# Moving sums of a fused attention and mixture-of-experts kernel from VectorE to GpSimd, with folding and packing on one two-bank PSUM tile

## The chip, the cores and the metric

The kernel runs on one core of one Trainium2 chip. Its engines are TensorE (PE, with its weight loads shown as PEld), VectorE (DVE), ScalarE (ACT), GpSimd (POOL) and SyncE (SP), which here only issues transfers. The metric is device time in microseconds; lower is better.

## The reference, cut to what matters

```python
batch, n_heads, seq, head_dim, n_pack = 8, 8, 576, 64, 32      # N, D, E, F = 4608, 512, 4, 1024

def sm_attn(qq, kk, vv):
    s = scale * np.matmul(qq, kk.transpose(0, 1, 3, 2))
    a = np.exp(s - np.max(s, axis=-1, keepdims=True))
    a = a / (np.sum(a, axis=-1, keepdims=True) + 1e-09)
    return np.matmul(a, vv)

p_packed = sm_attn(p, k, v)                  # 32 packing vectors attend to 576 keys, per head
x = sm_attn(q, p_packed, p_packed)           # the tokens attend to the packed vectors
p = domain_probs / (domain_probs.sum(-1, keepdims=True) + 1e-09)
for e in range(E):
    out += p[:, e:e + 1] * (np.maximum(x @ w1[e], 0.0) @ w2[e])
```

All of it is float32. An image is one entry of the batch: 576 tokens, 8 heads.

## The kernel before

**The work.** The token attention's result is never formed. The packed vectors are folded into the first weights instead (`g_form`: packed vectors times `w1`, per head), and the token probabilities (`xs`) are multiplied with that. The second matrix product is done with Winograd's form of Strassen's scheme: 2x2 blocks, seven products in the order `ORDER = ["a11", "s3", "s1", "s2", "a22", "s4", "a12"]`, with sums of the activation blocks (`s1` to `s4`, VectorE, line 316), sums of the weight blocks (`t1` to `t4`, line 354) and sums of the results (`finish`, line 391). Every operand of a large matmul is split into a high and a low part: the high part is a cast on ScalarE (`hi_of`, line 110), the low part a subtraction on GpSimd or VectorE (`lo_of`, line 115), and three matmuls make one product.

**The loops.** The main loop runs over `units`: four image pairs (`sb`), eight chunks of 512 hidden features (`ch`, two to an expert), and the two images of the pair, the even one first. A unit does the seven products of its chunk; between them it does four groups of matmuls for the next unit's hidden blocks (`mm1_group`, after products 1, 3, 4 and 6, evicted on VectorE at line 299 with ReLU and the token's expert probability). A product's PSUM tile is copied to an accumulator (ScalarE, line 380, chunk 0), added to it (VectorE, line 382, chunks 1 to 6) or handed to `finish` (chunk 7), which forms the block sums on VectorE and stores the four output blocks. The operand of product i+2 (`s_operand`) is prepared while product i runs; it lands in a tile `st`, of which there are four (`bufs=4`). The large PSUM tiles `dbl` are three of two banks each; the small ones `aux` are two of one bank.

**Beside them.** In even units the folding for the next chunk comes after products 2 and 5 (`next(gsteps)`), each step filling one `aux` tile per image. The next image pair's attention is spread over the loop as `back`: one packing unit (`pack_unit`, half the heads of one image) in each even unit of chunks 1 to 4, one token unit (`tok_unit`) in the even units of chunks 5 and 6 and in both units of chunk 7. A generator's `yield` ends the part done in one product step. In the first image pair, odd units also form the next chunk's weight operands (`t_form`), which `t_store` then saves to DRAM for the later image pairs (`t_load`).

**The start.** Before the loop, the first two images' packing and token units, the first folding and the first weight sums run interleaved. `norm_probs` loads the expert probabilities `dp`, normalises them on VectorE and stores them to DRAM (`pnd`), from where `load_probs` reads them back broadcast to all partitions. All transfers are issued on SP's queue.

**The order.** The order of instructions on TensorE is written by hand in part (`together`, `on_pe`). Otherwise each engine's order and all waits come from a scheduler that goes through the program with estimated durations and may bring an instruction forward that is ready; each engine then runs its list in order.

Of the kernel before, what the change touches and what calls it, by code (L numbers as in the profile page):

```python
# [16 lines left out]
P = 128  # L17
# [21 lines left out]
def attention_moe(ctx: ExitStack, tc: tile.TileContext, q, k, v, p, dp, w1, w2, out):  # L39
# [12 lines left out]
    ps_aux = pool("ps_aux", 2, space=PSUM)  # L52
# [30 lines left out]
    def aux():  # L83
        return ps_aux.tile([P, 512], F32, name="aux")
# [32 lines left out]
    def norm_probs():  # L117
        pb = const.tile([P, E, TP], F32, name="pb")
        nc.sync.dma_start(out=pb, in_=dp)
        ps = const.tile([P, TP, 1], F32, name="psum_e")  # L120
        nc.vector.tensor_reduce(out=ps, in_=pb.rearrange("p e t -> p t e"), axis=AX.X, op=ALU.add)
        nc.vector.tensor_scalar_add(ps, ps, 1e-9)
        nc.vector.reciprocal(out=ps, in_=ps)
        nc.vector.tensor_tensor(
            out=pb, in0=pb, in1=ps.rearrange("p t o -> p o t").broadcast_to([P, E, TP]), op=ALU.mult
        )
        nc.sync.dma_start(out=pnd.rearrange("e (p t) -> p e t", p=P), in_=pb)

    def pack_unit(b, g, new):
        pd = pbd[b % 2]  # L130
        if g == 0:
            pt = small.tile([P, NPAIR, NPK], F32, name="pt", bufs=1)
            nc.sync.dma_start(out=pt, in_=p[b])
            for hh in range(2):
                nc.gpsimd.tensor_copy(
                    out=pd[hh * D:(hh + 1) * D, :, hh * NPK:(hh + 1) * NPK], in_=pt[hh * D:(hh + 1) * D]
                )
        kt = new([P, 2, S], "kt")
        nc.sync.dma_start(out=kt, in_=k[b][:, 2 * g:2 * g + 2, :])
        vt = new([P, len(SC), 4 * D], "vt")  # L140
# [31 lines left out]
        for c in range(nfull):  # L172
            tr(out=ps[:, c * P:(c + 1) * P], in_=a1[:, c * P:(c + 1) * P], identity=ident)
        nc.scalar.copy(out=at[:, 0:nfull, :], in_=ps.rearrange("p (c s) -> p c s", s=P))
        ps = aux()
        r = S - nfull * P
        tr(out=ps[0:r, 0:P], in_=a1[:, nfull * P:S], identity=ident)
        nc.scalar.copy(out=at[0:r, nfull, :], in_=ps[0:r, 0:P])
        yield
        ps = aux()  # L180
        for c, (_, n) in enumerate(SC):
            for h in range(4):
                mm(
                    out=ps[h * NPK:(h + 1) * NPK, 0:D], lhsT=at[0:n, c, h * NPK:(h + 1) * NPK],
# [3 lines left out]
        nc.vector.tensor_scalar_mul(ppn, ps[:, 0:D], rs)  # L188
        yield
        ps = aux()  # L190
        tr(out=ps[0:D, 0:P], in_=ppn, identity=ident)
        psv = ps[0:D, 0:P].rearrange("p (j h n) -> p j h n", j=2, h=2)
# [9 lines left out]
    def tok_unit(b, g, new):  # L202
# [20 lines left out]
        nc.vector.tensor_tensor(out=a2, in0=a2, in1=m2.broadcast_to([P, S // 32, NPK]), op=ALU.subtract)  # L223
# [6 lines left out]
        nc.vector.tensor_tensor(out=a2, in0=a2, in1=s2.broadcast_to([P, S // 32, NPK]), op=ALU.mult)  # L230
# [18 lines left out]
    def g_form(bs, ch, raws):  # L249

        for g in range(NG):
            pss = {b: aux() for b in bs}
# [81 lines left out]
    def t_form(ch, new, eng):  # L334
# [15 lines left out]
        for i, name in enumerate(ORDER):  # L350
            n = of[name]
            if n in how:
                t = new([P, 2, DH], {"t1": "at", "t2": "a1", "t3": "a1", "t4": "at"}[n])
                eng.tensor_tensor(out=t, in0=blk[how[n][0]], in1=blk[how[n][1]], op=ALU.subtract)
# [31 lines left out]
    def finish(b, name, psv):  # L386
# [5 lines left out]

        def store(t, r, n):
# [12 lines left out]
        if name == "a11":  # L406
            add(m["s2"], m["s2"], t)
            add(m["a12"], m["a12"], t)
        elif name == "s2":
            add(m["s3"], m["s3"], t)  # L410
            add(m["s4"], m["s4"], t)
            add(m["s4"], m["s4"], m["s1"])
            add(m["s1"], m["s1"], m["s3"])
# [31 lines left out]
    with ExitStack() as first:  # L445
# [10 lines left out]
        toks = [tok_unit(b, g, unit_tile(2 * b + g)) for b in range(2) for g in range(NG)]  # L456
        forms = t_form(0, form_tile, nc.gpsimd)
        for i in range(2):
# [6 lines left out]
        for i in range(2, 4):  # L465
            next(packs[i])
        norm_probs()
        next(forms)
        drain(wavefront(packs[:2], 1))
        for b in range(2):  # L470
            load_probs(b, 0)
# [19 lines left out]
    for u, (sb, ch, b) in enumerate(units):  # L491
# [3 lines left out]
        back = nothing  # L495
        if sb + 1 < SB:
# [5 lines left out]
            elif ch == 7:  # L502
                back = tok_unit(nb + 1, b % 2, att_tile)
# [6 lines left out]
        tsteps = t_form(ch + 1, att_tile, nc.vector) if forming else nothing  # L510
        next(tsteps, None)
        for i in range(NPROD):
# [12 lines left out]
            next(back, None)  # L525
            next(tsteps, None)
# [4 lines left out]
        drain(back)  # L531
# [39 lines left out]
```

## Time and profile before

| | |
|---|---|
| median of three timed runs | 1383.59 us (1379.76 to 1385.15) |
| profiled execution | 1386.64 us |
| its span, first to last instruction | 1384.9 us |
| TensorE, weight loads | busy 1312.6 us (95%), 1192.3 us (86%) |
| VectorE, ScalarE, GpSimd | busy 984.0 us (71%), 475.0 us (34%), 804.0 us (58%) |
| transfers | 208.92 MB, mean 151 GB/s |
| TensorE's granted clock, mean over the span | 0.982 of full speed |

The share of an engine is an average over stages with different limits; the stretches of time in the rows below split it. A row of instructions names line, engine, operation and `out<-in` by the program's tiles, then shape and count. Idle time before an instruction is put down to what released it last.

### The profile page before, as it was taken

Reading aid. Unit: us, or ns where it says so; the run is one execution under the profiler, and the core shown is the slowest. Engines: PE = TensorE matmul, PEld = TensorE weight load, DVE = VectorE, ACT = ScalarE, POOL = GpSimd, SP = SyncE. Lnnn points to the kernel's source line nnn. Section 1 sums busy time; section 2 is a strip of 40 time slices with the busy share of each in tenths; the row PEclk is TensorE's granted clock in tenths of the full one; section 3 lists DMA queues with packets and bytes.
Section 4 is the critical chain, followed back from the end, with each engine's and each line's share of the span. In section 5 each row is a group of like instructions: output and inputs, shape, how many; then the busy total and the mean of one; then the engine's idle time right before and its main releaser. Section 6 shows DMA issues by size and latency. Waiting matters only on the chain.

```text
span 1384.9 us, 26088 instructions
## 1 busy us (share of the span) xinstructions
PE 1312.6 (95%) x10464; PEld 1192.3 (86%) x10464; DVE 984.0 (71%) x1380; ACT 475.0 (34%) x786; POOL 804.0 (58%) x548
## 2 busy tenths in 40 slices
PE   5699999999889999999998999999998899999997
PEld 2488898888888889899987998889997799999997
DVE  4757778788994666667798466666779656666668
ACT  2354343434325333233323433333332342332331
POOL 2656887777846445555645544455565455555555
PEclk9789999999999999999999999999999999999999
DMA  8525454444553444444445443445444344443421
GB/s 279 209 94 176 169 183 168 166 166 143 182 188 122 144 145 158 157 159 144 132 152 174 133 164 135 133 139 163 148 146 151 111 145 132 146 146 131 138 92 69
DMA packets 84630, 208.92 MB, mean 151 GB/s; under 512 B 8608, under 2 KB 27168, under 8 KB 84512
## 3 DMA queue, kind: packets, MB, share of 16 engines
q1 hardware_dynamic: 84512, 207.27, 44.5%
q8 instruction: 83, 1.36, 0.4%
q14 instruction: 35, 0.29, 0.1%
HBM read 168.37 MB, written 38.87 MB: 150 GB/s over the span
## 4 chain that ended last, share of the span: by engine, by line
PE 76%; DVE 16%; DMA 3%; issue 2%; POOL 1%; ACT 1%; DVEq 0%; SPq 0%; ACTq 0%
PE dbl L67 71%; DVE acc L391 5%; PE aux L75 4%; DVE sblk L316 4%; DVE ablk L299 2%; DMA kt<-in_w 1%; DVE ghl L115 1%; DVE acc L382 1%; DVE a L223 1%; DMA pb<-in_dp 1%; POOL xl L115 1%; PE aux L70 1%; DMA kt<-in_q 1%; DVE s L227 0%; DVE a L219 0%
## 5 line engine op out<-in xcount | busy, mean ns | idle before, releaser
L67 PEld LDWEIGHTS dbl<-st,tt 128*128 128x128 f32 x5376 | 736.1, 189 | 93.1 <-issue 61.4
L67 PE MATMUL dbl<-st,tt 128*128 128x288 f32 x5376 | 791.3, 299 | 23.2 <-DVE acc L391 6.6
L115 POOL TENSOR_TENSOR st<-sblk,st 128x576 fp32r<-128x576 f32 x256 | 397.7, 1559 | 292.3 <-ACT st L110 288.5
L67 PE MATMUL dbl<-xh,ghl 128*128 128x288 f32 x2048 | 419.8, 297 | 0.0
L115 POOL TENSOR_TENSOR st<-ablk,st 128x576 fp32r<-128x576 f32 x192 | 286.3, 1491 | 228.4 <-ACT st L110 193.1
L67 PEld LDWEIGHTS dbl<-xh,ghl 128*128 128x128 f32 x2048 | 333.4, 191 | 0.0
L299 DVE SCALAR_TENSOR_TENSOR ablk<-dbl,pbt 128x576 f32<-128x576 f32 x256 | 192.6, 752 | 188.8 <-PE dbl L67 188.7
L67 PE MATMUL dbl<-xl,ghl 128*128 128x288 f32 x1024 | 306.5, 299 | 17.3 <-POOL xl L115 15.5
L382 DVE TENSOR_TENSOR acc<-dbl,acc 128x576 f32<-128x576 f32 x336 | 253.2, 754 | 90.3 <-PE dbl L67 89.4
L110 ACT CAST st<-sblk 128x576 fp32r<-128x576 f32 x256 | 173.0, 676 | 356.3 <-DVE sblk L316 232.3
L110 ACT CAST st<-ablk 128x576 fp32r<-128x576 f32 x192 | 129.7, 675 | 261.6 <-PE dbl L67 241.2
L67 PEld LDWEIGHTS dbl<-xl,ghl 128*128 128x128 f32 x1024 | 195.2, 191 | 20.1 <-POOL xl L115 16.7
L316 DVE TENSOR_TENSOR sblk<-ablk 128x576 f32<-128x576 f32 x128 | 116.0, 906 | 10.7 <-POOL st L115 0.5
L115 DVE TENSOR_TENSOR ghl<-aux,ghl 128x512 fp32r<-128x512 f32 x128 | 83.3, 684 | 53.1 <-ACT ghl L110 53.1
L75 PE MATMUL aux<-wraw,ppbd 64*32 64x512 f32 x1024 | 85.9, 621 | 1.9 <-DVE ppbd L195 1.8
L110 ACT CAST ghl<-aux 128x512 fp32r<-128x512 f32 x128 | 69.0, 588 | 49.9 <-PE aux L75 49.9
L316 DVE TENSOR_TENSOR sblk<-ablk,sblk 128x576 f32<-128x576 f32 x64 | 65.4, 1022 | 6.5 <-POOL st L115 0.8
L391 DVE TENSOR_TENSOR acc<-acc,acc 128x576 f32<-128x576 f32 x56 | 58.1, 1069 | 0.2
L316 DVE TENSOR_TENSOR sblk<-sblk,ablk 128x576 f32<-128x576 f32 x64 | 55.7, 871 | 2.0
L380 ACT COPY acc<-dbl 128x576 f32<-128x576 f32 x56 | 35.7, 639 | 57.3 <-PE dbl L67 57.3
L391 DVE TENSOR_TENSOR acc<-dbl,acc 128x576 f32<-128x576 f32 x48 | 35.4, 742 | 1.7 <-PE dbl L67 1.7
L75 PEld LDWEIGHTS aux<-wraw,ppbd 64*32 64x32 f32 x1024 | 14.3, 106 | 23.4 <-issue 15.5
(66 smaller groups left out, 496.2 us busy)
## 6 DMA issues: line engine op xcount, KB each, us to landing
tt<-td SPq DMA_DIRECT2D x168, 512.0 KB, 3.8
wraw<-in_w SPq DMA_DIRECT2D x128, 256.0 KB, 3.0
td<-tt SPq DMA_DIRECT2D x56, 512.0 KB, 2.6
kt<-in_k SPq DMA_DIRECT2D x16, 576.0 KB, 3.8
kt<-in_q SPq DMA_DIRECT2D x16, 576.0 KB, 3.6
pbt<-pnd SPq DMA_DIRECT2D x32, 288.0 KB, 3.9
out<-acc SPq DMA_DIRECT2D x32, 288.0 KB, 2.6
vt<-in_v SPq DMA_DIRECT2D x16, 512.0 KB, 3.8
```

Of the source, the lines that this page charges most:

```text
L67: on_pe(nc.tensor.matmul(**kw))
L70: on_pe(nc.tensor.transpose(**kw))
L75: ins = nc.tensor.matmul(**kw).ins
L110: nc.scalar.copy(out=dst, in_=src)
L115: eng.tensor_tensor(out=dst, in0=src, in1=hi.bitcast(F32), op=ALU.subtract)
L223: nc.vector.tensor_tensor(out=a2, in0=a2, in1=m2.broadcast_to([P, S // 32, NPK]), op=ALU.subtract)
L299: nc.vector.scalar_tensor_tensor(out=a, in0=ps[:, :, 0:HS], scalar=0.0, in1=pbt[b][:, ts].rearrange("p (o t) -> p o t", o=1).broadcast_to( ...
L316: nc.vector.tensor_tensor(out=t, in0=blk(x), in1=blk(y), op=op)
L380: nc.scalar.copy(out=accs[b, i], in_=psv)
L382: nc.vector.tensor_tensor(out=accs[b, i], in0=psv, in1=accs[b, i], op=ALU.add)
L391: nc.vector.tensor_tensor(out=dst, in0=x, in1=y, op=op)
```

## The change

Folding and packing take their PSUM from one tile of two banks in place of two tiles of one bank. A folding step uses one bank for each image of the pair; packing puts the four full transposes into the first bank and the short one into the second before both are copied out. The expert probabilities are loaded and normalised first, with transfers issued on ScalarE's queue; the key loads of two packing units go ahead of their value loads, for which `pack_unit` has one more `yield`. The packing vectors are copied on ScalarE in place of GpSimd. In the start, the second token unit has its subtraction and its multiplication on GpSimd. The weight sums `t1` and `t3` go from VectorE to GpSimd. In `finish`, the sums in which both operands are accumulators go to GpSimd (`side`), except for the last image, and the two additions to `s4` change places. At chunk 7, the two token units of an image form one chain over both units, without a drain between them, so that the second begins in the even unit.

```diff
-    ps_aux = pool("ps_aux", 2, space=PSUM)
+    ps_aux = pool("ps_aux", 1, space=PSUM)
...
-        return ps_aux.tile([P, 512], F32, name="aux")
+        return ps_aux.tile([P, 2, 512], F32, name="aux")
...
     def norm_probs():
         pb = const.tile([P, E, TP], F32, name="pb")
-        nc.sync.dma_start(out=pb, in_=dp)
+        nc.scalar.dma_start(out=pb, in_=dp)
...
-        nc.sync.dma_start(out=pnd.rearrange("e (p t) -> p e t", p=P), in_=pb)
+        nc.scalar.dma_start(out=pnd.rearrange("e (p t) -> p e t", p=P), in_=pb)
...
-                nc.gpsimd.tensor_copy(
+                nc.scalar.copy(
                     out=pd[hh * D:(hh + 1) * D, :, hh * NPK:(hh + 1) * NPK], in_=pt[hh * D:(hh + 1) * D]
...
         nc.sync.dma_start(out=kt, in_=k[b][:, 2 * g:2 * g + 2, :])
+        yield
         vt = new([P, len(SC), 4 * D], "vt")
...
-            tr(out=ps[:, c * P:(c + 1) * P], in_=a1[:, c * P:(c + 1) * P], identity=ident)
-        nc.scalar.copy(out=at[:, 0:nfull, :], in_=ps.rearrange("p (c s) -> p c s", s=P))
-        ps = aux()
+            tr(out=ps[:, 0, c * P:(c + 1) * P], in_=a1[:, c * P:(c + 1) * P], identity=ident)
         r = S - nfull * P
-        tr(out=ps[0:r, 0:P], in_=a1[:, nfull * P:S], identity=ident)
-        nc.scalar.copy(out=at[0:r, nfull, :], in_=ps[0:r, 0:P])
+        tr(out=ps[0:r, 1, 0:P], in_=a1[:, nfull * P:S], identity=ident)
+        nc.scalar.copy(out=at[:, 0:nfull, :], in_=ps[:, 0].rearrange("p (c s) -> p c s", s=P))
+        nc.scalar.copy(out=at[0:r, nfull, :], in_=ps[0:r, 1, 0:P])
...
-    def tok_unit(b, g, new):
+    def tok_unit(b, g, new, eng=nc.vector):
...
-        nc.vector.tensor_tensor(out=a2, in0=a2, in1=m2.broadcast_to([P, S // 32, NPK]), op=ALU.subtract)
+        eng.tensor_tensor(out=a2, in0=a2, in1=m2.broadcast_to([P, S // 32, NPK]), op=ALU.subtract)
...
-        nc.vector.tensor_tensor(out=a2, in0=a2, in1=s2.broadcast_to([P, S // 32, NPK]), op=ALU.mult)
+        eng.tensor_tensor(out=a2, in0=a2, in1=s2.broadcast_to([P, S // 32, NPK]), op=ALU.mult)
...
         for g in range(NG):
-            pss = {b: aux() for b in bs}
+            ps = aux()
+            pss = {b: ps[:, b % 2] for b in bs}
...
-                eng.tensor_tensor(out=t, in0=blk[how[n][0]], in1=blk[how[n][1]], op=ALU.subtract)
+                eng[n].tensor_tensor(out=t, in0=blk[how[n][0]], in1=blk[how[n][1]], op=ALU.subtract)
...
+        def side(dst, x, y, op=ALU.add):
+            (nc.vector if b == B - 1 else nc.gpsimd).tensor_tensor(out=dst, in0=x, in1=y, op=op)
+
...
         if name == "a11":
-            add(m["s2"], m["s2"], t)
-            add(m["a12"], m["a12"], t)
+            side(m["s2"], m["s2"], t)
+            side(m["a12"], m["a12"], t)
         elif name == "s2":
-            add(m["s3"], m["s3"], t)
-            add(m["s4"], m["s4"], t)
-            add(m["s4"], m["s4"], m["s1"])
-            add(m["s1"], m["s1"], m["s3"])
+            side(m["s3"], m["s3"], t)
+            side(m["s4"], m["s4"], m["s1"])
+            side(m["s4"], m["s4"], t)
+            side(m["s1"], m["s1"], m["s3"])
...
-        toks = [tok_unit(b, g, unit_tile(2 * b + g)) for b in range(2) for g in range(NG)]
-        forms = t_form(0, form_tile, nc.gpsimd)
-        for i in range(2):
+        toks = [
+            tok_unit(b, g, unit_tile(2 * b + g), nc.gpsimd if (b, g) == (0, 1) else nc.vector)
+            for b in range(2) for g in range(NG)
+        ]
+        forms = t_form(0, form_tile, {n: nc.gpsimd for n in ("t1", "t2", "t3", "t4")})
+        norm_probs()
+        for i in (0, 1, 0, 1):
             next(packs[i])
...
-        for i in range(2, 4):
+        for i in (2, 3, 2, 3):
             next(packs[i])
-        norm_probs()
+        for b in range(2):
+            load_probs(b, 0)
...
-        back = nothing
+        if not (ch == 7 and odd):
+            back = nothing
...
-            elif ch == 7:
-                back = tok_unit(nb + 1, b % 2, att_tile)
+            elif ch == 7 and not odd:
+                back = chain(*[tok_unit(nb + 1, g, att_tile) for g in range(NG)])
...
-        tsteps = t_form(ch + 1, att_tile, nc.vector) if forming else nothing
+        tsteps = t_form(ch + 1, att_tile, {"t1": nc.gpsimd, "t2": nc.vector, "t3": nc.gpsimd, "t4": nc.vector}) if forming else nothing
...
             next(back, None)
+            if i == 0 and ch <= 4:
+                next(back, None)
...
-        drain(back)
+        if not (ch == 7 and not odd):
+            drain(back)
```

## Rows read from the trace of the kernel before

**Rows 1.** The page, busy time of each engine, its share of the span and its instructions.

```profile
PE 1312.6 (95%) x10464; PEld 1192.3 (86%) x10464; DVE 984.0 (71%) x1380; ACT 475.0 (34%) x786; POOL 804.0 (58%) x548
```

**Rows 2.** The page, the chain of work that ended last, shares of the span by engine.

```profile
PE 76%; DVE 16%; DMA 3%; issue 2%; POOL 1%; ACT 1%; DVEq 0%; SPq 0%; ACTq 0%
```

**Rows 3.** Busy time in stretches of the span (us from its start): length, then each engine's busy us and its number of instructions, then TensorE's granted clock, the share of the DMA engines, GB/s. From the top: the start; an odd unit of the first image pair that forms weight sums; a pair of units with a packing unit; one with a token unit; the pair at the end of the second image pair; the pair after it; a pair with nothing beside it; the last pair.

```profile
0.00:71.00 71.00, 40.60 (x353) 26.07 (x353) 42.84 (x85) 22.90 (x44) 34.72 (x37) 0.85 0.70 238
...
302.00:324.50 22.50, 19.95 (x139) 19.75 (x138) 20.84 (x23) 8.30 (x15) 20.21 (x14) 0.92 0.44 159
...
588.00:629.70 41.70, 41.54 (x355) 37.47 (x356) 27.25 (x42) 12.41 (x22) 20.44 (x14) 1.00 0.45 149
629.70:668.60 38.90, 38.90 (x313) 36.10 (x320) 29.32 (x43) 12.65 (x20) 23.29 (x15) 1.00 0.46 147
...
707.40:756.70 49.30, 41.20 (x313) 36.46 (x316) 45.49 (x59) 16.08 (x26) 26.78 (x17) 0.99 0.51 173
...
756.70:796.80 40.10, 40.10 (x313) 36.47 (x320) 18.36 (x26) 17.50 (x30) 19.53 (x14) 0.97 0.40 130
...
1129.60:1167.10 37.50, 37.50 (x304) 35.49 (x310) 24.82 (x34) 11.61 (x18) 20.86 (x14) 1.00 0.42 135
1348.00:1384.90 36.90, 29.60 (x219) 28.95 (x218) 31.36 (x38) 6.75 (x10) 19.42 (x11) 0.94 0.19 65
```

**Rows 4.** Groups of instructions in the stretch 707.4 to 756.7 us: line, engine, operation, tiles, shape and count, then busy us, mean ns of one, and idle time before them with its releaser.

```profile
L115 POOL TENSOR_TENSOR st<-sblk,st 128x576 fp32r<-128x576 f32 x8 | 13.1, 1647 | 15.3 <-ACT st L110 15.3
L391 DVE TENSOR_TENSOR acc<-acc,acc 128x576 f32<-128x576 f32 x12 | 11.6, 997 | 0.0
L115 POOL TENSOR_TENSOR st<-ablk,st 128x576 fp32r<-128x576 f32 x7 | 11.1, 1585 | 7.6 <-ACT st L110 7.6
...
L115 POOL TENSOR_TENSOR xl<-at,xh 128x576 fp32r<-128x576 f32 x2 | 3.7, 1866 | 0.9 <-ACT xh L110 0.9
```

**Rows 5.** Who waited for whom in the stretch 707.4 to 756.7 us: total us, times, longest us.

```profile
POOL st L115 <- ACT st L110: 22.9, 9, 5.5
...
PE dbl L67 <- DVE ablk L299: 2.3, 2, 2.0
...
PE dbl L67 <- DVE acc L391: 2.1, 3, 1.5
PE dbl L67 <- POOL xl L115: 2.0, 1, 2.0
```

**Rows 6.** Single instructions of the last pair in order of time: start us, us, engine, line, operation.

```profile
1355.62 1.44 POOL L115 TENSOR_TENSOR st<-ablk,st 128x576 fp32r<-128x576 f32 x1 [0.82 <-ACT st L110]
...
1357.20 2.67 DVE L391 TENSOR_TENSOR acc<-acc,acc 128x576 f32<-128x576 f32 x2
1357.21 2.05 POOL L115 TENSOR_TENSOR st<-ablk,st 128x576 fp32r<-128x576 f32 x1 [0.15 <-ACT st L110]
...
1360.46 1.41 DVE L391 TENSOR_TENSOR acc<-acc,acc 128x576 f32<-128x576 f32 x2
...
1375.13 3.43 PE L67 MATMUL dbl<-st,tt 128*128 128x288 f32 x24 [0.42 <-DVE acc L391]
```

**Rows 7.** Weight sums: the groups of the whole span on VectorE (`t1`, `t3`) and on GpSimd (in the start), then, from the view of waits, those of TensorE and of its weight loads in the stretch 292 to 377 us, which has the last two pairs that form weight sums.

```profile
L354 DVE TENSOR_TENSOR at<-kt 128x512 f32<-128x512 f32 x7 | 7.3, 1037 | 1.3 <-POOL xl L115 1.3
L354 DVE TENSOR_TENSOR a<-vt,kt 128x512 f32<-128x512 f32 x7 | 5.6, 799 | 2.8 <-DMA vt<-in_w 2.8
L354 POOL TENSOR_TENSOR sblk<-st 128x512 f32<-128x512 f32 x2 | 3.1, 1552 | 0.0
...
PE dbl L67 <- DVE acc L382: 5.1, 2, 2.5
...
PEld dbl L67 <- POOL st L115: 7.6, 5, 2.8
```

**Rows 8.** Instructions of the start in order of time.

```profile
5.13 2.19 PE L67 MATMUL dbl<-kt,pbd 128*64 128x288 f32 x8 [5.13 <-DMA kt<-in_k]
9.01 2.19 PE L67 MATMUL dbl<-kt,pbd 128*64 128x288 f32 x8 [1.69 <-DMA kt<-in_k]
...
15.29 0.26 ACT L178 COPY at<-aux 64x128 f32<-64x128 f32 x1
15.66 0.59 SPq L119 DMA_DIRECT2D pb<-in_dp  x1
25.51 0.40 DVE L121 TENSOR_REDUCE psum_e<-pb 128x36 f32<-128x144 f32 x1 [1.64 <-DMA pb<-in_dp]
27.54 1.28 DVE L124 TENSOR_TENSOR pb<-pb,psum_e 128x144 f32<-128x144 f32 x1
33.92 1.52 DVE L223 TENSOR_TENSOR a<-a,m 128x576 f32<-128x576 f32 x1
46.82 1.40 POOL L115 TENSOR_TENSOR xl<-at,xh 128x576 fp32r<-128x576 f32 x1
```

**Rows 9.** The small PSUM tiles in a pair with a packing unit, in order of time: the read-out of the first folding step, the transposes, the packing copies, the next folding step.

```profile
589.73 1.29 DVE L115 TENSOR_TENSOR ghl<-aux,ghl 128x512 fp32r<-128x512 f32 x2 [0.70 <-ACT ghl L110]
593.02 0.60 PE L70 MATMUL aux<-ident,a 128*128 128x128 f32 x4
599.13 2.00 PE L75 MATMUL aux<-wraw,ppbd 64*32 64x512 f32 x16
599.46 0.44 DVE L195 COPY ppbd<-aux 64x64 f32<-64x64 f32 x2
```

More of the change, by code (lines that the diff above doesn't have):

```diff
@@ L183, in pack_unit @@
                 mm(
-                    out=ps[h * NPK:(h + 1) * NPK, 0:D], lhsT=at[0:n, c, h * NPK:(h + 1) * NPK],
+                    out=ps[h * NPK:(h + 1) * NPK, 0, 0:D], lhsT=at[0:n, c, h * NPK:(h + 1) * NPK],
                     rhs=vt[0:n, c, h * D:(h + 1) * D], start=c == 0, stop=c == len(SC) - 1,
@@ L187, in pack_unit @@
         ppn = small.tile([P, D], F32, name="ppn")
-        nc.vector.tensor_scalar_mul(ppn, ps[:, 0:D], rs)
+        nc.vector.tensor_scalar_mul(ppn, ps[:, 0, 0:D], rs)
         yield
         ps = aux()
-        tr(out=ps[0:D, 0:P], in_=ppn, identity=ident)
-        psv = ps[0:D, 0:P].rearrange("p (j h n) -> p j h n", j=2, h=2)
+        tr(out=ps[0:D, 0, 0:P], in_=ppn, identity=ident)
+        psv = ps[0:D, 0, 0:P].rearrange("p (j h n) -> p j h n", j=2, h=2)
         prs = slice(2 * g, 2 * g + 2)
@@ L464, in attention_moe @@
             next(toks[i])
-        for i in range(2, 4):
+        for i in (2, 3, 2, 3):
             next(packs[i])
-        norm_probs()
+        for b in range(2):
+            load_probs(b, 0)
         next(forms)
         drain(wavefront(packs[:2], 1))
-        for b in range(2):
-            load_probs(b, 0)
         drain(g_form([0], 0, raws))
```

## Prediction, made before the change was run

> **What bounds the kernel now.** I read the page first, then busy time by stretch, then the slowest stretch by group of instructions and by wait, then single instructions in order of time. TensorE is busy 95% of the span [rows 1], and the chain that ended last runs 76% on TensorE and 16% on VectorE [rows 2]. So the time is TensorE's own work plus the places where it waits; the reader should look for those places, because the matmuls themselves are not changed.
>
> The stretches show them [rows 3]. A pair of units (two images, one chunk of hidden features) with nothing beside it lasts 37.5 us. A pair with one token unit lasts 38.9, so a token unit costs 1.4 of TensorE. A pair with a packing unit lasts 41.7, and TensorE is busy 41.54 of it: that is its own work and not a wait. The pair at the end of an image pair lasts 49.3. It has two token units, so 37.5 + 2 x 1.4 = 40.3 would do, and **9.0 us are lost**, three times in the run. VectorE is busy 45.5 of those 49.3 us there, GpSimd only 26.8. The start is the other loss: 71 us, with TensorE busy 40.6 and its clock at 0.85 of full speed on average.
>
> Inside the slow pair [rows 4], 12 additions of accumulators (both operands in SBUF, 997 ns) take 11.6 us of VectorE, and 17 subtractions take 27.9 us of GpSimd (13.1 + 11.1 + 3.7, the windows' 26.8 counts no overlap twice). The waits [rows 5] say the same: TensorE waits there for VectorE's blocks (2.3), its sums (2.1) and GpSimd's token parts (2.0), while GpSimd sits 22.9 us for operands that ScalarE gets late from VectorE.
>
> **Sums at the end of a pair, and the token units' order (the main term).** For three boundaries the 12 additions leave VectorE: 45.5 - 11.6 = 33.9 us, no longer a bound. They join GpSimd's queue. No row shows such an add on GpSimd; the nearest are its subtractions of the same 128x576 shape: 1.44 us alone, 2.05 beside a VectorE op with two SBUF operands [rows 6], 26.8/17 = 1.58 on average in this stretch [rows 3, 4]. I take 1.58, since as many additions leave VectorE as come to GpSimd. GpSimd then has 29 x 1.58 = 45.8 us (41.8 at 1.44, 59.5 at 2.05), more than TensorE's 40.3. It need not all fit: the next pair has GpSimd busy 19.5 of 40.1 [rows 3]. What sits behind the new additions in GpSimd's queue are the `st` low parts for the next products, and TensorE waits for these; a burst of four (6.3 us) comes behind product `s2`. Four `st` buffers let it lag by two or three products (1.7 us each: 24 matmuls, two products, in 3.43 [rows 6]). VectorE in turn waits in order: `a22` needs GpSimd's `s3`, `s4` its third sum, and each holds one of three PSUM tiles. I take 45.8 less 2.0 that runs over into the next pair: **43.8 us, a gain of 5.5 per boundary, 16.5 in all**. Bounds: 8.2 each if the pair reaches 41.1, which is TensorE's floor and 0.8; a loss of 0.3 each if nothing runs over and the twelve cost 1.9 (26.8 + 22.8 = 49.6). The token chain starts its second unit two products earlier; that takes away the 2.0 us wait for token parts [rows 5], which is inside the 5.5.
>
> Last pair of the run: image 6 gives six additions to GpSimd, busy there 19.4 of 36.9; image 7 keeps its own on VectorE. TensorE is busy 29.6 of the 36.9 [rows 3], and its last matmuls end at 1375.13 + 3.43 = 1378.56 [rows 6], 6.3 before the span's end; so only about 1.0 of waiting lies before image 7's closing sums, which do not move. **0**, from -1 (that wait gone) to +2 (a `st` low part behind the burst).
>
> Here a rule of the Trainium skill speaks against the change. "SBUF — State Buffer", section "SBUF: two separate sides", says VectorE with two SBUF inputs and GpSimd share one port pair as an exclusive lock, so that the loser is fully blocked. Rows nearly bear that out: two such VectorE additions take 1.41 alone and GpSimd's subtraction 1.44, together 2.85, and side by side they needed 2.67 [rows 6]. By the rule the boundary's lock time would be 29 x 1.44 + 12 two-operand VectorE operations that stay (eight block sums, four of the token units) x 0.71 (half of 1.41) = 50.3 us, so no gain without running over: 1367 + 16.5 + 3 x 1.0 = 1386. Rival 1 below has this mechanism, priced by rows.
>
> **Weight sums, first image pair, seven pairs.** `t1` and `t3` leave VectorE: 1.04 + 0.80 = 1.84 us per pair. GpSimd gains two of 1.55 (its own such subtractions in the start) [rows 7], 3.1. In these odd units GpSimd already shows 20.2 of 22.5 us busy, VectorE 20.8 [rows 3]. Over the last two such pairs TensorE waited 5.1 us for VectorE and its weight loads 7.6 for GpSimd [rows 7]. So a wait is exchanged: I give half of the 5.1 back as gain (-2.5), and charge 0.7 us per pair for a fuller GpSimd (+5): **+2.5**. Bounds: -3 (GpSimd absorbs it in the even unit, all but 2 of the 5.1 gone) and +14 (2 per pair). `t2` on VectorE now waits for `t1` on GpSimd, and behind it stand PSUM additions.
>
> **Start.** The probabilities' load is issued at 15.66 us on SP's queue, after all four packing units' loads, lands at 25.5, and VectorE idled 1.64 for it; the two large ones of its four operations then take 0.40 + 1.28 = 1.68 of VectorE just as token work begins [rows 8]. Loaded first and on ScalarE's queue, both leave that place: -3.3 us. The second token unit gives a subtraction (1.52 on VectorE) and a multiplication to GpSimd, where they meet the first weight sums; its low part already waited there until 46.82 behind three others [rows 8]: +1.5. Keys before values: the second packing's scores came at 9.01, waiting for keys; they can come about 2 us earlier, and the second queries with them, -2. Against this ScalarE's queue now holds the store of normalised probabilities, which waits for VectorE, ahead of the two copies of packing vectors, and the first scores at 5.13 wait for these: +0.5 (0 if the copies are placed first, up to 3). The first units' packing now shares one folding tile, a wait of one short copy (0.26): +0.3. Sum **-3**, bounds -8 (all gains and a warmer clock) and +3.
>
> **One two-bank tile.** In a steady packing pair the folding results are read out by 591.02 and the transposes come at 593.02; the next folding at 599.13 waited for the packing copy that ends at 599.90 anyway [rows 9]. I cost it at nothing. If that slack is gone, it is a wait for one more read-out, 0.2 us for each of 16 units: +3 at most. Packing's copies on ScalarE in the steady state are 12, at 0.26 for the nearest row, a 64x128 copy [rows 8], on an engine busy 12.4 of 41.7 [rows 3]: nothing, as its slack hides them; without it 3.1.
>
> **Sum.** -16.5 + 0 + 2.5 - 3 + 0 = -17.0 us. The profiled execution took 1386.64 us, of which 1384.9 is span; 1369.6 is the forecast for it. It lay 3.05 above the median of the three timed runs (1383.59), so the forecast against that median is 1366.6, **1367**.
>
> **Rivals.**
> 1. *GpSimd's path is the bound*: it runs its operations at their price beside VectorE's. Its place is the pair at the end of an image pair. With nothing running over, the 29 GpSimd operations fit the old 49.3 us only below 1.70 us each. At 1.58 with VectorE blocked in addition, the boundaries stay at 49.3: 1367 + 16.5 = 1383. At 1.9, 29 x 1.9 = 55.1: +5.8 each, 1367 + 16.5 + 17.4 = 1401, **slower**. For it: 2.05 beside VectorE, 45.8 above TensorE's floor. Against it: half of the next pair is free, and twelve colliding operations fewer on VectorE. 0.16, split evenly.
> 2. *Weight sums fill GpSimd*: every odd unit of the first image pair is GpSimd-bound and loses the whole 3.1, 21.7 instead of 2.5: 1386. For it: 20.2 of 22.5. Against: the even units have it half idle. 0.10, of which 0.02 slower.
> 3. *Everything hidden*: boundaries at 41.1 (-24.6), last pair -1, start -8, weights 0: -33.6, 1350. For it: `st` can be made up to four ahead. 0.14.
>
> The forecast has 0.60, its own range 1354 to 1378. From these: a change under 0.5% (7 us) is not told from none; faster 0.72 (0.58 of the forecast's 0.60, and 0.14), same 0.18 (0.02 + 0.08 + 0.08), slower 0.10. The range 1348 to 1387 leaves out half of rival 1 and the far ends.
>
> **What the profile after would show.** Boundary pairs of about 44 us, VectorE there near 34 busy, GpSimd near 44; the wait for token parts before the pair's end gone; sums on GpSimd at about 1.6 us. If they read 1.9, or weight loads wait for `st` low parts by many us, rival 1 holds. Odd units of the first image pair above 22.5 us show rival 2. The start's stretch should end near 68 us instead of 71. The prediction is wrong if VectorE, freed of 11.6 us, is held as long by waits for GpSimd's sums.

## The result, and the profile after

The change made the kernel **slower: 1394.07 us against 1383.59** (medians of five runs each; ratio 1.0079, 95% interval 1.0057 to 1.0101). The forecast was 1367, its range 1348 to 1387.

The profiled execution took 1395.93 us, 1393.8 of it span. The page's busy line and the shares of the chain that ended last answer to [rows 1, 2]:

```profile
PE 1310.0 (94%) x10464; PEld 1202.4 (86%) x10464; DVE 960.1 (69%) x1322; ACT 483.0 (35%) x802; POOL 882.6 (63%) x590
...
PE 76%; POOL 9%; DVE 8%; DMA 3%; issue 3%; ACT 1%; DVEq 0%; SPq 0%; ACTq 0%; POOLq 0%
```

VectorE was relieved, its share of the chain fell from 16% to 8%, and GpSimd's rose from 1% to 9%. The stretches that answer to [rows 3] (columns as there; each is moved by the shift of the work it covers: the start to 12 us after the first product, the boundary pair, the pair after it, the last pair):

```profile
0.00:75.60 75.60, 44.21 (x353) 27.42 (x354) 42.37 (x82) 25.78 (x53) 33.04 (x32) 0.72 0.65 223
714.30:764.70 50.40, 44.15 (x333) 40.06 (x333) 39.25 (x50) 17.18 (x28) 43.02 (x28) 0.93 0.52 172
764.70:801.00 36.30, 36.30 (x286) 34.34 (x292) 17.51 (x24) 16.81 (x29) 18.75 (x14) 1.00 0.42 140
1352.30:1393.80 41.50, 32.04 (x220) 31.57 (x218) 28.22 (x32) 6.75 (x10) 26.80 (x17) 0.89 0.17 58
```

The boundary pair was to fall to 43.8 us and stands at 50.4, though part of that is the edge of the window: it and the pair after it take 86.7 together where they took 89.4. VectorE fell to 39.3 busy (forecast 34) and GpSimd rose to 43.0 (forecast 44). The last pair grew, and so did the start, with its clock at 0.72. Groups in the boundary pair, as [rows 4], and its waits, as [rows 5]:

```profile
L395 POOL TENSOR_TENSOR acc<-acc,acc 128x576 f32<-128x576 f32 x10 | 16.7, 1684 | 0.0
...
L392 DVE TENSOR_TENSOR acc<-acc,acc 128x576 f32<-128x576 f32 x2 | 3.9, 1958 | 1.3 <-POOL acc L395 1.3
```

```profile
PEld dbl L67 <- DVE acc L392: 4.5, 1, 4.5
PE dbl L67 <- DVE acc L392: 4.5, 2, 4.3
```

A sum on GpSimd took 1.68 us, not 1.58, and the two subtractions for `a22` left on VectorE took 1.96. TensorE's three longest waits of [rows 5], 1.5 to 2.0 us, are gone; one of 4.3 us is there instead. In order of time it reads so (start us, us, engine, line, operation, in brackets the idle time and its releaser; other rows left out):

```profile
745.22 1.95 POOL L395 TENSOR_TENSOR acc<-acc,acc 128x576 f32<-128x576 f32 x1
...
747.13 1.40 POOL L115 TENSOR_TENSOR xl<-at,xh 128x576 fp32r<-128x576 f32 x1
747.20 1.94 DVE L392 TENSOR_TENSOR acc<-acc,acc 128x576 f32<-128x576 f32 x1 [1.33 <-POOL acc L395]
...
748.49 1.91 POOL L395 TENSOR_TENSOR acc<-acc,acc 128x576 f32<-128x576 f32 x1
749.07 1.95 DVE L317 TENSOR_TENSOR sblk<-sblk,ablk 128x576 f32<-128x576 f32 x1
...
750.94 0.74 DVE L392 TENSOR_TENSOR acc<-acc,dbl 128x576 f32<-128x576 f32 x1
...
751.73 0.61 PE L67 MATMUL dbl<-xl,ghl 128*128 128x288 f32 x1 [4.30 <-DVE acc L392]
```

VectorE waits 1.33 us for GpSimd's sum into `s3`, then its own two operations run at 1.94 and 1.95, and only then does it read the PSUM tile that TensorE needs. The clock falls within that wait (busy time of TensorE, its weight loads, VectorE, ScalarE and GpSimd in each stretch, then the granted clock):

```profile
740.50:747.40 6.90, 6.90 (x52) 6.69 (x51) 5.20 (x8) 2.03 (x3) 6.90 (x5) 1.00 0.60 195
747.40:751.80 4.40, 0.10 (x2) 0.07 (x1) 4.40 (x4) 0.67 (x1) 4.40 (x3) 0.77 0.59 205
751.80:756.60 4.80, 4.80 (x20) 4.80 (x21) 2.69 (x4) 0.00 (x0) 4.59 (x4) 0.50 0.71 246
```

TensorE did nothing for 4.3 us and then ran its next 4.8 us at 0.50, the lower of its two clocks (1.2 GHz). So a wait is paid for twice. In what follows, "at half clock" is time with a granted clock of 0.50; it is taken to lose up to half of itself (here 20 matmuls in 4.8 us, against 52 in the 6.9 us at full clock).

The other difference is the folding tile. In a packing pair of after:

```profile
812.41 0.30 PE L70 MATMUL aux<-ident,ppn 128*64 128x128 f32 x1 [0.88 <-DVE ppn L188]
812.75 0.45 DVE L195 COPY ppbd<-aux 64x64 f32<-64x64 f32 x2 [0.39 <-PE aux L70]
...
813.30 1.09 PE L75 MATMUL aux<-wraw,ppbd 64*32 64x512 f32 x16 [0.58 <-PE aux L70]
...
814.33 3.05 PE L67 MATMUL dbl<-st,tt 128*128 128x288 f32 x12
...
814.51 0.59 ACT L110 CAST ghl<-aux 128x512 fp32r<-128x512 f32 x1 [2.96 <-PE aux L75]
815.13 0.69 DVE L115 TENSOR_TENSOR ghl<-aux,ghl 128x512 fp32r<-128x512 f32 x1 [1.93 <-ACT ghl L110]
815.86 0.58 ACT L110 CAST ghl<-aux 128x512 fp32r<-128x512 f32 x1 [0.76 <-DVE ghl L115]
```

The second image's read-out by ScalarE waits until VectorE has read the first image's bank of the same tile; before, VectorE's two subtractions ran directly one behind the other, 1.29 us together [rows 9]. And TensorE now stands 0.88 and 0.58 us around the packing steps.

Taken pair by pair over the whole run (pairs of units counted from 0, from the first matmul of each pair's products in the two traces), after differs from before by +4.6 us at the first product, -0.8 over pairs 0 to 6 of the first image pair, -5.1 at the three boundaries (each with the pair behind it), +5.6 in the eight packing pairs of the later image pairs, and +4.7 in the last pair: +9.0.

### The profile page after: what moved, and what is told of

It reads as the page before. It is cut to its first block, busy times and chain, and to the rows that moved or that the text cites. A ratio compares the mean times of both kernels' runs of the same rounds, so it can differ in the third digit from the quotient of the medians.

```text
span 1393.8 us, 26088 instructions
## 1 busy us (share of the span) xinstructions
PE 1310.0 (94%) x10464; PEld 1202.4 (86%) x10464; DVE 960.1 (69%) x1322; ACT 483.0 (35%) x802; POOL 882.6 (63%) x590
## 4 chain that ended last, share of the span: by engine, by line
PE 76%; POOL 9%; DVE 8%; DMA 3%; issue 3%; ACT 1%; DVEq 0%; SPq 0%; ACTq 0%; POOLq 0%
PE dbl L67 72%; PE aux L75 4%; POOL st L115 3%; DVE sblk L317 3%; POOL tt L115 2%; POOL acc L395 2%; DVE acc L392 2%; DMA kt<-in_w 1%; DVE ablk L300 1%; DMA st<-in_w 1%; PE aux L70 1%; DMA pnd<-pb 1%; POOL xl L115 1%; DVE ghl L115 1%; DVE acc L395 0%
## 5 line engine op out<-in xcount | busy, mean ns | idle before, releaser
L67 PE MATMUL dbl<-xh,ghl 128*128 128x288 f32 x2048 | 424.4, 299 | 0.0
L67 PEld LDWEIGHTS dbl<-xl,ghl 128*128 128x128 f32 x1024 | 196.9, 192 | 28.2 <-DVE acc L392 17.1
L115 DVE TENSOR_TENSOR ghl<-aux,ghl 128x512 fp32r<-128x512 f32 x128 | 87.9, 687 | 72.5 <-ACT ghl L110 72.2
L317 DVE TENSOR_TENSOR sblk<-ablk 128x576 f32<-128x576 f32 x128 | 123.2, 962 | 11.0 <-DVE ablk L300 1.4
L110 ACT CAST ghl<-aux 128x512 fp32r<-128x512 f32 x128 | 74.8, 584 | 88.7 <-PE aux L75 54.4
L75 PE MATMUL aux<-wraw,ppbd 64*32 64x512 f32 x1024 | 74.2, 612 | 11.3 <-PE aux L70 5.3
L395 POOL TENSOR_TENSOR acc<-acc,acc 128x576 f32<-128x576 f32 x42 | 69.1, 1657 | 0.0
L317 DVE TENSOR_TENSOR sblk<-ablk,sblk 128x576 f32<-128x576 f32 x64 | 60.7, 948 | 6.5 <-POOL st L115 0.3
L317 DVE TENSOR_TENSOR sblk<-sblk,ablk 128x576 f32<-128x576 f32 x64 | 63.8, 997 | 1.6
L115 POOL TENSOR_TENSOR xl<-at,xh 128x576 fp32r<-128x576 f32 x16 | 26.4, 1652 | 16.2 <-ACT xh L110 16.2
```

The source lines that it names most:

```text
L67: on_pe(nc.tensor.matmul(**kw))
L75: ins = nc.tensor.matmul(**kw).ins
L110: nc.scalar.copy(out=dst, in_=src)
L115: eng.tensor_tensor(out=dst, in0=src, in1=hi.bitcast(F32), op=ALU.subtract)
L317: nc.vector.tensor_tensor(out=t, in0=blk(x), in1=blk(y), op=op)
L395: (nc.vector if b == B - 1 else nc.gpsimd).tensor_tensor(out=dst, in0=x, in1=y, op=op)
```

## Experiments

All medians below come with the kernel before run on the same chip; the ratio is to that one. In every run whose edit has `side`, but for the start alone, the two additions to `s4` stand in their changed order. The four ends of the argument first: the change without one or both of its suspects.

**Two tiles back** (all else as in the changed kernel).

```
-    ps_aux = pool("ps_aux", 1, space=PSUM)
+    ps_aux = pool("ps_aux", 2, space=PSUM)
-        return ps_aux.tile([P, 2, 512], F32, name="aux")
+        return ps_aux.tile([P, 512], F32, name="aux")
...
-            ps = aux()
-            pss = {b: ps[:, b % 2] for b in bs}
+            pss = {b: aux() for b in bs}
```

> The changed kernel with the two one-bank folding tiles of the kernel before put back; all else stays changed. Theory A (the single two-bank tile is the large loss: by the lengths of the pairs in the two traces about +4 in the start, +5.6 in the eight longest packing pairs of the second and third block, +3.7 in the first block): 1394 - 13 = 1381 us, and the half-clock stretches inside the packing pairs are gone. Theory B (the sums on GpSimd are the loss, and the tile is worth nothing): about 1393 us.

Measured 1381.3 us (0.9993, 0.9979 to 1.0007): 12.8 us of the loss was the tile. The packing pairs stand at 41.77 again, all eight.

**The tile alone** on the kernel before (the same lines the other way, with the packing steps written for two banks).

> The kernel before with nothing changed but the folding tiles: one two-bank tile, with the read-outs and the weight-folding step written as in the changed kernel. Theory A (the tile costs about 13 us wherever it stands): 1396 us, packing pairs 0.3 to 1.8 us longer each and the first product of the main loop about 4 us later. Theory B (the tile alone costs nothing): 1384 us.

Measured 1408.8 us (1.0191, 1.0167 to 1.0215): 25.6 us, twice what was expected. The first product comes 8.2 us later than in the kernel before and pairs 1 to 4 are 2.3 to 4.0 us longer each. The rows that tell it are the groups of ScalarE's read-outs, with two tiles (the kernel before) and then with one (this run); the last columns are ScalarE's idle time before them and who ended it:

```profile
L110 ACT CAST ghl<-aux 128x512 fp32r<-128x512 f32 x128 | 69.0, 588 | 49.9 <-PE aux L75 49.9
```

```profile
L110 ACT CAST ghl<-aux 128x512 fp32r<-128x512 f32 x128 | 74.9, 585 | 106.4 <-PE aux L75 71.8 <-DVE ghl L115 34.4
```

With one tile ScalarE waits 34.4 us for VectorE's reads of it (34.1 in the changed kernel); with two, not at all.

**All sums back on VectorE** (the rest as in the changed kernel, one tile).

```
-            (nc.vector if b == B - 1 else nc.gpsimd).tensor_tensor(out=dst, in0=x, in1=y, op=op)
+            nc.vector.tensor_tensor(out=dst, in0=x, in1=y, op=op)
```

> The changed kernel with all end-of-pair sums back on VectorE (in the changed order); the two-bank tile, the start and the weight sums stay changed. Theory A (boundaries lose the 5 us, the end regains 4.7): 1394 us, the last pair back at about 30.3 us from 35.0. Theory B (the sums are the loss): 1383 us. If the longer wait at the boundaries comes from the token steps' new place rather than from the sums, the boundaries stay where they are and the end alone regains: 1389 us.

Measured 1383.2 us (1.0000, 0.9985 to 1.0015). My first theory had no change; this is the second's time, and 10.9 us came back: in the traces the last pair its 4.5, the boundaries 6.5. So the sums on GpSimd, the main gain of the forecast, are a loss in this kernel.

**Both undone** (two tiles, sums on VectorE; start, weight sums and token order changed).

> The changed kernel with both suspects undone: the two one-bank folding tiles are back and all end-of-pair sums are on VectorE; start, weight sums and the order of the token steps stay changed. If the two losses are separate (12.8 us for the tile, from the run with two tiles; 10.9 us for the sums, from the run with the sums on VectorE): 1394 - 12.8 - 10.9 = 1370 us, faster than both kernels. If they are one loss seen twice (the half clock that either idle time triggers): about 1381 us.

Measured **1370.7 us (0.9916, 0.9898 to 0.9934)**: the two losses are separate, and this version is faster than both kernels. From it the way to the changed kernel is +10.5 for the sums (1381.3) and +12.8 for the tile (1394.1).

Next, each remaining part alone on the kernel before.

**Sums alone, for all images but the last; then for six of eight.**

```
+        def side(dst, x, y, op=ALU.add):
+            (nc.vector if b == B - 1 else nc.gpsimd).tensor_tensor(out=dst, in0=x, in1=y, op=op)
...
-            add(m["s2"], m["s2"], t)
+            side(m["s2"], m["s2"], t)
```

(and so the other five, the two additions to `s4` exchanged; in the second run `b >= B - 2`)

> The kernel before with nothing changed but the end-of-pair sums: on GpSimd for all images but the last, in the changed kernel's order. Theory A (by the pairs' lengths the boundaries gain 5 us and the last two images' end loses 4.7): 1383 us, no change beyond 0.5 %. Theory B (the sums on GpSimd cost about 10 us): 1394 us. The forecast on record would give 1367 to 1370 us.

> The kernel before with nothing changed but the end-of-pair sums, on GpSimd for the first six images (the last two on VectorE). Theory A (the last pair lost 3.6 us to GpSimd, the three boundaries gained 9 to 10): 1380.4 - 3.6 = 1377 us. Theory B (the last pair's lengthening is a clock dip that has nothing to do with the sums): 1380 us.

Measured 1380.4 us (0.9985, 0.9969 to 1.0000) and 1376.2 us (0.9952, 0.9936 to 0.9968). The 4.1 us between them come with image 6, whose sums lengthen the last pair from 30.3 to 34.0 us in the first run's trace, with a wait of TensorE of 3.3 us; in the second it is 30.5, and no wait there is over 1 us.

**The token order alone.**

```
-        back = nothing
+        if not (ch == 7 and odd):
+            back = nothing
...
-            elif ch == 7:
-                back = tok_unit(nb + 1, b % 2, att_tile)
+            elif ch == 7 and not odd:
+                back = chain(*[tok_unit(nb + 1, g, att_tile) for g in range(NG)])
...
-        drain(back)
+        if not (ch == 7 and not odd):
+            drain(back)
```

> The kernel before with nothing changed but the order of the token steps around the end of a block: the two token units of the second image in one chain over the last two units of the block, not drained in between. If the gain of the run with both suspects undone sits at the boundaries (its three pairs of boundary and next pair are 1.3, 4.5 and 4.6 us shorter than before's): 1383.5 - 8 to 10 = 1374 to 1376 us. If that gain came from VectorE's relief elsewhere: 1383 us.

Measured 1376.2 us (0.9947, 0.9932 to 0.9961), as expected. I had booked only a 2 us wait for it.

**The token order and the sums of six images together**, nothing else.

> The kernel before with the new order of the token steps and the end-of-pair sums of the first six images on GpSimd, nothing else. Each alone brought 7.4 to 7.6 us. Theory A (the two spoil one another directly: the token units' own GpSimd work now falls between the sums): 1380 to 1386 us, slower than either alone. Theory B (they add: the loss seen with both needs the other parts of the change): 1369 us. Theory C (they take the same stall away, so the second brings nothing): 1376 us.

Measured 1382.7 us (1.0000, 0.9990 to 1.0010): each alone brings 7.4 to 7.6 us, both together nothing that can be told from none. The same sequence as in the changed kernel is in this trace:

```profile
1069.80 1.95 POOL L394 TENSOR_TENSOR acc<-acc,acc 128x576 f32<-128x576 f32 x1
...
1071.70 1.40 POOL L115 TENSOR_TENSOR xl<-at,xh 128x576 fp32r<-128x576 f32 x1
1071.78 1.94 DVE L391 TENSOR_TENSOR acc<-acc,acc 128x576 f32<-128x576 f32 x1 [1.33 <-POOL acc L394]
1073.06 1.91 POOL L394 TENSOR_TENSOR acc<-acc,acc 128x576 f32<-128x576 f32 x1
...
1076.31 0.61 PE L67 MATMUL dbl<-xl,ghl 128*128 128x288 f32 x1 [4.30 <-DVE acc L391]
```

and the stretch behind it, its clock at 0.50:

```profile
1074.80:1081.60 6.80, 5.29 (x22) 5.29 (x23) 4.67 (x6) 0.67 (x1) 6.17 (x5) 0.50 0.54 189
```

Between the sum into `s3`, for which VectorE waits, and the next sum on GpSimd stands the token unit's `xl`, which the new order brings forward; VectorE's subtraction runs beside it. The following table, from the traces, sums the three boundary pairs with the pair behind each (us; "idle" is the length less TensorE's busy time; the last column, an estimate, is the length less half of the time at half clock):

| kernel | length | TensorE idle | at half clock | less half of it |
|---|---|---|---|---|
| before | 267.5 | 24.3 | 10.2 | 262.4 |
| sums of six images alone | 257.6 | 18.9 | 6.8 | 254.2 |
| token order alone | 258.8 | 20.6 | 3.4 | 257.1 |
| both | 263.3 | 22.3 | 17.1 | 254.8 |
| changed kernel, two tiles, sums on VectorE | 257.1 | 17.7 | 3.4 | 255.4 |
| changed kernel, two tiles | 265.3 | 23.2 | 20.5 | 255.1 |
| changed kernel | 262.4 | 20.2 | 20.5 | 252.2 |

In the last column either part takes the same 5 to 8 us, once; the second adds next to nothing. What it adds is one long wait (2.4 us with the token order alone, 3.2 with the sums alone, 4.3 with both) and with it two and a half to five times the time at half clock. So of the three theories both the first and the third seem to have a part: the gain is had once, and the second way to it costs clock. As the last column is an estimate, this split is argued, not shown; the total is the first theory's.

**Only the sums that nothing waits for soon on GpSimd** (two tiles, new token order, six images).

```
-            side(m["s3"], m["s3"], t)
+            add(m["s3"], m["s3"], t)
             side(m["s4"], m["s4"], m["s1"])
-            side(m["s4"], m["s4"], t)
+            add(m["s4"], m["s4"], t)
```

> The changed kernel with two one-bank folding tiles, and on GpSimd only those end-of-pair sums that no later product waits for soon (s2 += a11, a12 += a11, s4 += s1, s1 += s3), of the first six images; s3 += s2 and the second sum of s4, on which the products a22 and s4 wait, are on VectorE, and so are all sums of the last two images. Theory A (the loss is the way of the two urgent sums over GpSimd's queue): within 2 us of the run with all sums on VectorE, or 2 us below it, 1368 to 1371 us. Theory B (any sum on GpSimd costs, by the dearer VectorE instructions beside it): 1375 us or more.

Measured 1380.4 us (0.9976, 0.9963 to 0.9990), which speaks for theory B: the last pair is back at 30.5, but the boundaries take 265.5 us with waits of 3.3 to 3.6 us and 23.9 us at half clock. It is not the queue of the urgent sums alone: ahead of its 3.6 us wait VectorE waits for no sum of GpSimd, but two sums of its own take 3.20 us and a block sum 1.95 beside GpSimd's work.

**The old token order in the changed kernel** (two tiles, sums of six images on GpSimd), and the same with the sums on VectorE, which is the start and the weight sums, with the two additions to `s4` exchanged. Against the changed kernel, beside the tile lines of the first run:

```
-            elif ch == 7 and not odd:
-                back = chain(*[tok_unit(nb + 1, g, att_tile) for g in range(NG)])
+            elif ch == 7:
+                back = tok_unit(nb + 1, b % 2, att_tile)
...
-            (nc.vector if b == B - 1 else nc.gpsimd).tensor_tensor(out=dst, in0=x, in1=y, op=op)
+            (nc.vector if b >= B - 2 else nc.gpsimd).tensor_tensor(out=dst, in0=x, in1=y, op=op)
```

(in the second run `nc.vector` for all)

> The changed kernel with two one-bank folding tiles, the token steps in the order of the kernel before, and the end-of-pair sums on GpSimd for the first six images. Theory A (the sums on GpSimd and the new order of the token steps each shorten the boundaries and spoil one another): the sums' gain comes back, 7.6 us as when they were moved alone, with 4 to 6 us of start and weight sums: 1370 to 1373 us. Theory B (with the start and the weight sums changed, GpSimd has no room for the sums in either order): 1380 us.

> The kernel before with the new start and the weight sums on GpSimd; token steps, end-of-pair sums and the folding tiles as before. The parts alone brought 7.9 and 1.4 us. If they add: 1374 us; then the new order of the token steps brings 3 us on top (1370.7) and the sums on GpSimd nothing (1374.7). If the start's gain is partly the same clock luck as in the first block: 1378 us, and both bring more.

Measured 1374.7 us (0.9938, 0.9923 to 0.9952) and 1383.2 us (1.0002, 0.9989 to 1.0015). On top of the second, the sums bring 8.4 us, though the second has a wait of its own, shown below; on the kernel before they brought 7.6. So they do gain, as long as the token order is the old one. That the second run gives nothing, though the start alone gives 8, I had not expected:

**The start alone** (probabilities first and on ScalarE's queue, keys before values, the copies and two token operations moved); its core:

```
-        nc.sync.dma_start(out=pb, in_=dp)
+        nc.scalar.dma_start(out=pb, in_=dp)
...
-                nc.gpsimd.tensor_copy(
+                nc.scalar.copy(
...
+        norm_probs()
+        for i in (0, 1, 0, 1):
-        for i in range(2):
             next(packs[i])
...
-        norm_probs()
```

> The kernel before with nothing changed but the start: probabilities first and on ScalarE's queue, packing copies on ScalarE, two token operations of one unit on GpSimd, the packing unit's extra step. By the run with both suspects undone the first product of the second pair came 5.5 us earlier than in the kernel before (102.5 against 108.0): 1379 us. The forecast on record had 3 us for it: 1381 us. If the start is hidden behind its other loads: 1384 us.

Measured 1375.6 us (0.9950, 0.9931 to 0.9969). The first product comes 10.5 us earlier in the trace, the second pair's 7.5.

**The weight sums alone.**

```
-        tsteps = t_form(ch + 1, att_tile, nc.vector) if forming else nothing
+        tsteps = t_form(ch + 1, att_tile, {"t1": nc.gpsimd, "t2": nc.vector, "t3": nc.gpsimd, "t4": nc.vector}) if forming else nothing
```

> The kernel before with nothing changed but the weight differences of chunks 1 to 7: the first and third on GpSimd, the second and fourth on VectorE. Theory A (pairs 5 and 6 of the first block shorten by 2.1 and 1.8 us, the others stay): 1379 us. Theory B, the term of the forecast on record (GpSimd is the later of the two there): 1386 us.

Measured 1382.5 us (0.9995, 0.9981 to 1.0010): not told from none. Pairs 5 and 6 are 3.3 and 2.6 us shorter in its trace, pairs 1 to 4 0.5 to 1.3 us longer.

How the run of start and weight sums loses it again stands in its trace: VectorE's list has two sums ahead of the read of a PSUM tile.

```profile
723.18 3.83 DVE L395 TENSOR_TENSOR acc<-acc,acc 128x576 f32<-128x576 f32 x2
...
726.93 0.74 DVE L392 TENSOR_TENSOR acc<-dbl,acc 128x576 f32<-128x576 f32 x1
...
727.83 2.50 PE L67 MATMUL dbl<-st,tt 128*128 128x288 f32 x9 [3.79 <-DVE acc L392]
```

```profile
726.10:732.90 6.80, 5.08 (x21) 5.11 (x22) 5.57 (x9) 0.67 (x1) 1.31 (x2) 0.50 0.29 88
```

The second fence is the stretch around it, again at 0.50. The wait of 3.8 us is there at all three boundaries, with 6.8 us at half clock each; they take 271.3 us together, 7.0 more than with the start alone (264.3), where no wait is over 2.0 and the read comes ahead of the two sums:

```profile
720.40 0.74 DVE L392 TENSOR_TENSOR acc<-dbl,acc 128x576 f32<-128x576 f32 x1
721.07 3.18 DVE L395 TENSOR_TENSOR acc<-acc,acc 128x576 f32<-128x576 f32 x2
```

But the two parts are not all that is in this run: its two additions to `s4` are exchanged, while the start alone and the weight sums alone have them as in the kernel before, and in both of these traces the read comes first. Of the three edits only the exchange is one at the boundary, which makes it the first suspect; no run has it alone. So it is not shown that the start and the weight sums spoil one another.

**Packing on one of two banks** (the fastest version, with this edit).

```
-    def aux():
-        return ps_aux.tile([P, 512], F32, name="aux")
+    def aux(i=0):
+        return ps_aux.tile([P, 512], F32, name=f"aux{i % 2}")
...
-            pss = {b: aux() for b in bs}
+            pss = {b: aux(b + g) for b in bs}
```

> The fastest version so far (two one-bank folding tiles, sums on VectorE; 1370.7 us) with one thing changed: the packing unit's four uses all take the same one of the two banks, one after another, while the folding step still has a tile for each image. Theory A (the 12.5 us of the single two-bank tile come from the two images' read-outs being tied to one tile): 1371 us, packing pairs 41.8. Theory B (they come from packing's steps queueing on one tile): packing pairs 42.1 to 43.6 us, 1376 to 1383 us in all.

Measured 1371.8 us (0.9925, 0.9903 to 0.9948), not told from the 1370.7 without it. Each of the eight packing pairs is 0.33 us longer, so packing's queue for one bank is real and explains the 0.29 us that most of them lost with the single tile. It shows in the start too: in its trace the first product comes 5.4 us later than in the fastest version's, pair 5 3.4 and the last pair 5.2 later, though the medians are only 1.1 apart. With one tile for all uses and the sums on VectorE, the last pair comes 15.2 us later than in the fastest version's trace, and 11.9 of these lie before pair 5 of the first image pair. So packing's queue is some 1 to 5 us of the tile's 12.5. The rest is put down to folding, which no run had on one tile by itself; the rows for it are these. In the start one image is folded at a time, and the second folding step stood for the read-out of the first (after):

```profile
58.91 1.06 PE L75 MATMUL aux<-wraw,ppbd 64*32 64x512 f32 x8 [2.18 <-DVE ghl L115]
...
59.90 3.82 PE L67 MATMUL dbl<-kt,ppbd 128*64 128x288 f32 x16
```

where the fastest version folds both steps at once:

```profile
44.32 1.92 PE L75 MATMUL aux<-wraw,ppbd 64*32 64x512 f32 x16
```

## Why the prediction was wrong

- **One two-bank tile, costed at nothing, "+3 at most".** This is the step that failed most: 12.8 us here, 25.6 alone. I read the slack from [rows 9] and asked only whether the tile was free in time in a steady packing pair. That reading was loose too: the folding row begins at 599.13, before the end (599.90) of the copy for which I said that it waited. And I did not ask what else the tile's two banks tie together: the second image's read-out waits for the first's, and with one image, in the start, the second half is empty and there is no second tile to fold into. Each small wait was then priced at its own length, not at that of the half clock behind it: packing pairs lose 0.3 us without it and 1.8 with it.
- **Sums and token order, -16.5.** The direction of each was right: alone they bring 7.6 and 7.4 us, and a sum on GpSimd took 1.68 us, between the 1.58 I chose and the 1.70 at which rival 1 held. In the changed kernel the three boundaries gained 5.1 us in all. The step that failed is "a gain of 5.5 per boundary" out of busy sums. VectorE was no bound by its sum (39 of 50 us), but the chain `s3` on GpSimd, subtraction on VectorE, read of the PSUM tile was; I named it ("`a22` needs GpSimd's `s3`") and gave it no price. In the changed kernel it is 4.3 us of waiting and 6.8 at half clock at each boundary. The prediction's own sign of being wrong, that VectorE is "held as long by waits for GpSimd's sums", came true only in small: in the stretch it waited 1.3 us for them, and over the boundary pair and the pair behind it its busy time fell by 9.0 us of the 11.6 that left it. What counted was where the rest fell: 2.4 us of it are the chain's two operations, at 1.94 and 1.95 in place of 0.74 each.
- **The lock.** Beside GpSimd the two-operand operations of VectorE took 1.94 and 1.95 us; the same subtraction takes 0.74 with the sums on VectorE. The Trainium skill, "SBUF — State Buffer", section "SBUF: two separate sides", has a VectorE operation with two SBUF inputs and a GpSimd operation that reads SBUF hold one port pair by turns, each for its whole instruction. The trace nearly agrees: two of these operations took 3.89 us beside GpSimd's, where two of VectorE's alone (0.74) and two of GpSimd's alone (1.44) would make 4.36 in turn. What rival 1 had wrong is the place: the price fell on three operations in a chain (`s3` at 1.95 us, VectorE's two), while the 28 GpSimd operations of the stretch took 1.54 us on average.
- **Last pair, 0 (-1 to +2).** Measured +4.7: the same two VectorE operations at 1.98 and 1.95 us, behind them a wait of 3.3 us, and 6.8 us at half clock.
- **Weight sums, +2.5.** About -1.4, not told from none and inside its bounds; the pairs where [rows 7] showed the waits became shorter.
- **Start, -3.** Alone -7.9, the near bound; in the changed kernel the first product came 4.6 later than before, with two tiles 6.1 earlier. That the parts were independent was itself an unstated step: sums and token order bring 15.0 us if added and about 1 in one kernel, and over all parts the single runs add up to 25.6 (tile) - 2.9 (sums) - 7.4 (token order) - 1.4 (weight sums) - 7.9 (start) = +6.0, measured +10.5.

Left open: why a wait of one length is followed by half clock in one place and not in another; what the exchange of the two additions to `s4` does by itself; what folding on one tile costs without packing; and whether an order exists in which both boundary parts gain.

## What to carry to other kernels

When buffers are merged, list every pair of accesses that the merge orders, in every phase, the one that fills only half of the tile too; slack in one steady stage says nothing of the others. A busy engine is relieved by moving work only if the moved work is not in the chain that frees the bottleneck's buffers: walk the chain operation by operation, at the price beside the other engine. And price a wait of the matrix engine with the clock that follows it, measure parts alone and in pairs, and count even an exchange of two additions as a part.

## What the runs showed of the hardware that I had not expected

Long single waits of TensorE were mostly followed by a lower clock. In the sixteen traces, past the first 20 us of the main loop, 31 waits of TensorE lasted 3.0 us or longer; in 26 of them half clock began within the wait or soon behind it, for 5.1 us on average. Of 80 waits of 1.5 to 2.2 us it was so in 25, and of 131 of 0.8 to 1.5 us in 26. From the first product to the last, the changed kernel had 55 us at half clock, the kernel before 27 and the fastest version 15. This fits one wait of 4.3 us being worse than the three of 1.5 to 2.0 us that it replaced; that it is the cause of every difference between the runs is argued, not shown.
